# Attention and a routed expert layer on one core: the row steps of attention stand ahead of a task's products with V

## The chip, the cores and the metric
The kernel runs on one core of a Trainium2 chip. Its engines take their instructions from queues of their own and wait for each other through semaphores: TensorE (PE, matmuls; PEld its weight loads), VectorE (DVE), ScalarE (ACT), GpSimd (POOL) and SyncE (SP, which only issues DMAs here). The metric is the time of one execution on the device, in microseconds. Before the change the median of 3 runs is 685.51 us (685.28 to 686.04).

## The reference
Eight batches of 576 tokens and 8 heads of 64. The first four heads see the last 32 tokens, the other four every 32nd token. The rows of all batches, 4608 by 512, then go through a layer of 8 experts of which each token takes one.

```
scores = scale * np.matmul(q, k.transpose(0, 1, 3, 2))
mask_local = (rel >= 0) & (rel < stride)
mask_strided = (rel >= 0) & (pos[None, :] % stride == pos[:, None] % stride)
...
attn = np.exp(scores)
attn = attn / (np.sum(attn, axis=-1, keepdims=True) + 1e-09)
return np.matmul(attn, v).astype(np.float32)
...
logits = x @ w_gate
expert_idx = np.argmax(logits, axis=1)
...
    h = np.maximum(xe @ w1[e], 0.0)
    ye = h @ w2[e]
    out[mask] = gate_w[mask, None] * ye
```

## The kernel before
The work of attention is cut into 40 tasks (b, k): batch b of 8, bank k of 5. A bank is one PSUM bank that holds the scores of four pairs of blocks. Banks 0 and 1 are local heads, bank 3 and 4 strided ones, bank 2 has both. A loop over i works on three tasks at once: `stage_s` of task i (mask and scores, L354, L360, L369, then the softmax: maximum L316, subtraction L319, exponential L320, sum L322, reciprocal L324 and L325, and the normalization on GpSimd, L326), `stage_t` of task i − 2 (four transposes of the probabilities, L396, and a copy `pT`), and the products with V of task i − 3, where its bank completes something: `av_local` behind bank 1, `av_strided` behind banks 3 and 4 (L406). ScalarE copies the products into `xT`, the rows of x transposed (L113).

Two batches are a group of 9 blocks of 128 tokens. Behind the products of bank 4 of a batch, row steps go into a list: `logits` of each chunk of 384 tokens that is now complete (one behind the first batch of a group, two behind the second; L468, then transposes L475 and the gate, L476 to L490), `xrows` of each block (four transposes L460, a copy, a store to `xd` by ScalarE's queue, L463, with the gate that GpSimd copies beside it, L457), and behind the second batch `route` of the group: counts on TensorE (L508, L510), place and key of every token, two factors `am` and `bb` on VectorE (L534, L542, L544), and their product, L549, which adds the tokens' numbers to `idacc`. Each pass of the loop takes three steps from the list, in its last lines. In the list of group 2, behind `route`, stands `start_early`: three gathers (L184) of expert 0's first rows, so that its work may begin while the last group is routed.

The engines' queues are filled by a scheduler. It takes what the program issued first as the more urgent, and moves an instruction ahead of others where it expects the inputs of these later. So the place in the loop decides the order in the main, and not to the letter. PSUM banks `s` (scores, logits, rows of x, counts) are three that go round, `t` two, `v` three. Behind the loop, TensorE's order is written out by hand: the logits of the last group between the transposes and first matmuls of expert 0 (L220, L234 to L253). The experts' weights come in f32 and are split in two parts by ScalarE (L165) and VectorE (`wlo`, L166); from there on TensorE works through the experts to the end.

Of the kernel before, what the change touches and what calls it, by code (L numbers as in the profile page):

```python
# [43 lines left out]
LAG_AV = 3  # L44
# [45 lines left out]
def moe_attn(ctx, tc, lqk, vl, sqk, vs, wg, wcat, blob, out):  # L90
# [10 lines left out]
    def bank(tag):  # L101
        if tag in rings:
            rings[tag].append(rings[tag].pop(0))
            tag = rings[tag][-1]
        return ps.tile([128, 512], F32, name=tag)

    def evac(which, out, in_):
        if which == "v":
            nc.vector.tensor_copy(out=out, in_=in_)
        elif which == "g":  # L110
            nc.gpsimd.tensor_copy(out=out, in_=in_)
        else:
            nc.scalar.copy(out=out, in_=in_)  # L113
# [173 lines left out]
    with ExitStack() as actx:  # L287
# [43 lines left out]
        def load_l(b, hp):  # L331
            qk = inp.tile([128, LW], F32, name="lqk_sb")
            loaded[b, "l", hp] = qk
            nc.sync.dma_start(out=qk, in_=lqk[b, hp])

        def load_s(b, hp):
            qk = whl.tile([128, CHW], F32R, name="whi").bitcast(F32)[:, 0:2 * S]
            loaded[b, "s", hp] = qk
            nc.sync.dma_start(out=qk, in_=sqk[b, hp])

        def load_vl(b, hp):
            vt = inv.tile([128, NQB // 2, 128], F32, name="vt", bufs=3)
            loaded[b, "vl", hp] = vt
            nc.sync.dma_start(out=vt, in_=vl[b, :, hp])

        def load_vs(b):
            vst = inv.tile([128, NRG, 128], F32, name="vst")
            loaded[b, "vs"] = vst
            nc.sync.dma_start(out=vst, in_=vs[b])
# [43 lines left out]
        def stage_t(b, k, prob):  # L393
            tb = bank("t")
            for x in range(4):
                nc.tensor.transpose(tb[:, x * 128:(x + 1) * 128], prob[:, x * 128:(x + 1) * 128], ident)  # L396
            pT = pts.tile([128, 512], F32, name="pT")
            evac("a", pT, tb)
            pTs[b, k] = pT
# [8 lines left out]
        def av_local(b, xT, off):  # L408
            vt = [loaded[b, "vl", hp] for hp in range(2)]
            av = [bank("v"), bank("v")]  # L410
            for hp in range(2):
                for m in range(4):
                    for i in range(2):
                        n = 2 * m + i
                        for y in range(2):
                            for h in range(2):
                                av_mm(av[y], 256 * hp + QB * n, QB, h, y, vt[hp][64 * y:64 * y + 64, n, 64 * h:64 * h + 64],
                                      probs_of(b, ("l", hp, m), y, slice(64 * h + 32 * i, 64 * h + 32 * i + 32)))
            for y in range(2):
                dst = xT[:, 0:2, off:off + 512].rearrange("p a (n y q) -> p a n y q", y=2, q=QB)[:, :, :, y, :]  # L420
                evac("a", dst, av[y].rearrange("p (a n q) -> p a n q", a=2, q=QB))
# [43 lines left out]
        def logits(g, c3, xT, L):  # L465
            lb = bank(LTAG)
            for pr in range(4):
                nc.tensor.matmul(lb[32 * pr:32 * pr + 32, 0:384], wg_sb[:, pr, :], xT[:, pr, c3 * 384:(c3 + 1) * 384],  # L468
                                 start=True, stop=True, tile_position=(0, 32 * pr))
            ls = rt.tile([128, 384], F32, name="ls", bufs=2)  # L470
            evac(LS_ENG, ls, lb[:, 0:384])
            yield
            lt = bank(LTAG)
            for i in range(3):
                nc.tensor.transpose(lt[:, i * 128:(i + 1) * 128], ls[:, i * 128:(i + 1) * 128], ident)  # L475
            nc.vector.tensor_reduce(out=L[:, 3 * c3:3 * c3 + 3, :],  # L476
                                    in_=lt[:, 0:384].rearrange("p (t q e) -> p t e q", t=3, q=4)[:, :, 0:E, :],
                                    axis=AX.X, op=ALU.add)
            cs = slice(3 * c3, 3 * c3 + 3)
            mx = rt.tile([128, 3], F32, name="mx", bufs=2)  # L480
            nc.vector.tensor_reduce(out=mx, in_=L[:, cs, :], axis=AX.X, op=ALU.max)
            dl = dls[g][:, cs, :]
            nc.vector.tensor_tensor(out=dl, in0=L[:, cs, :], in1=mx.unsqueeze(2).broadcast_to([128, 3, E]), op=ALU.subtract)
            ex = rt.tile([128, 3, E], F32, name="ex", bufs=2)
            nc.scalar.activation(out=ex, in_=dl, func=AF.Exp)
            yield
            gt = gates[g][:, cs]
            nc.vector.tensor_reduce(out=gt, in_=ex, axis=AX.X, op=ALU.add)
            nc.vector.tensor_scalar(out=gt, in0=gt, scalar1=1e-9, scalar2=None, op0=ALU.add)
            nc.vector.reciprocal(out=gt, in_=gt)  # L490
# [85 lines left out]
        def one(fn, *a):  # L576
            fn(*a)
            yield

        def step():  # L580
            while queue:
                try:
                    next(queue[0])
                    return True
                except StopIteration:
                    queue.pop(0)
            return False
# [23 lines left out]
        nt = len(tasks)  # L611
        pvs = {}
        for i in range(nt + LAG_AV):
            if i < nt:
                b, k = tasks[i]
                pvs[i] = stage_s(b, k)
                if b + 1 < B:
                    if k in (0, 1):
                        load_l(b + 1, k)
                    elif k in (3, 4):  # L620
                        load_s(b + 1, k - 3)
            it = i - LAG_T
            if 0 <= it < nt:
                stage_t(*tasks[it], pvs.pop(it))
            ia = i - LAG_AV
            if 0 <= ia < nt:
                b, k = tasks[ia]
                g, bb = divmod(b, GB)
                if g not in xTs:
                    xTs[g] = xtp.tile([128, 4, GB * S], F32, name="xT")  # L630
                    Ls[g] = rt.tile([128, GT, E], F32, name="L", bufs=2)
                    dls[g] = rt.tile([128, GT, E], F32, name="dl", bufs=2)
                    gates[g] = rt.tile([128, GT], F32, name="gt", bufs=2)
                if k == 1:
                    av_local(b, xTs[g], bb * S)
                elif k == 3:
                    av_strided(b, 0, xTs[g], bb * S)
                    if b + 1 < B:
                        load_vl(b + 1, 0)
                        load_vl(b + 1, 1)  # L640
                elif k == 4:
                    av_strided(b, 1, xTs[g], bb * S)
                    if b + 1 < B:
                        load_vs(b + 1)
                    for c3 in range(bb, 1 if bb == 0 else GT // 3):
                        queue.append(logits(g, c3, xTs[g], Ls[g]))
                    for c in range(3 * bb, 3 if bb == 0 else GT):
                        queue.append(one(xrows, g, c, xTs[g]))
                    if bb == GB - 1:
                        queue.append(route(g))  # L650
                        if g == NG - 2:
                            queue.append(one(start_early))
            if i < nt + LAG_AV - 1:
                for _ in range(3):
                    step()
        early = holder[0]
        lga, lgb = queue[0:2]
        rows = queue[2:8]
# [310 lines left out]
def build(nc, tc, aps):  # L969
    moe_attn(tc, *[aps[n] for n in _INS], aps["out"])  # L970
# [20 lines left out]
```

## Time and profile before

| | |
|---|---|
| median of 3 runs | 685.51 us |
| the profiled execution | 689.96 us, span 688.2 us |
| TensorE busy, mean granted clock | 641.9 us (93%), 0.967 |
| VectorE, ScalarE, GpSimd busy | 405.5, 319.1, 142.7 us |
| attention | 0 to some 201 us; the experts after it |

The page gives busy times over the whole span; the table of stretches gives them by stage, with the clock that TensorE was granted (1.00 is 2.4 GHz, and the other of its two levels is half of it). In the order of time a row is a run of equal instructions: start, length, engine, line, what it writes and reads, how many, and in brackets the idle time of the engine before it and what ended that. A bracket with "issue" is idle time that ended with no semaphore that the profile shows. Matmuls overlap, so rows of TensorE may overlap too.

### The profile page before, as it was taken

The numbers are of one execution on the slowest core, as the hardware profiler recorded it, in microseconds if no ns is written. First come the engines' busy times: TensorE is split into PE (matmuls) and PEld (weight loads), VectorE is DVE, ScalarE is ACT, GpSimd is POOL, SyncE is SP. The second block draws the span as 40 slices with busy tenths as digits, with TensorE's granted clock in tenths as the row PEclk, the third lists the DMA queues.
The fourth block names the chain that finished last, engine by engine and source line by source line (L and its number), as shares of the span: only waits on it lengthen the run. The fifth ranks groups of instructions, "written<-read, shape, count | busy, mean of one in ns | idle before, by whom it ended". The sixth has DMA issues, their size and how long they took to land.

```text
span 688.2 us, 15915 instructions
## 1 busy us (share of the span) xinstructions
PE 641.9 (93%) x6692; PEld 523.0 (76%) x6692; DVE 405.5 (59%) x762; ACT 319.1 (46%) x537; POOL 142.7 (21%) x163
## 2 busy tenths in 40 slices
PE   4898799899879999999999999999999999999992
PEld 3665677668659888888888888888888888888881
DVE  4564767867947984466646656456565556543320
ACT  1353545656733633355545455545555455534220
POOL 1321222332413060231123103301240124001102
PEclk9797999999989999999999999999999999999996
DMA  9386976776245674655575646654675566312301
GB/s 344 137 268 242 326 272 231 272 273 207 84 169 185 267 264 144 215 210 196 195 258 192 228 168 253 230 213 163 231 257 196 183 230 232 117 62 81 106 0 62
DMA packets 30217, 137.01 MB, mean 199 GB/s; under 512 B 4669, under 2 KB 4669, under 8 KB 21440
## 3 DMA queue, kind: packets, MB, share of 16 engines
q1 hardware_dynamic: 17856, 105.65, 43.0%
q0 software_dynamic: 6432, 20.26, 8.6%
q10 hardware_dynamic: 5856, 10.07, 3.9%
q8 instruction: 53, 0.87, 0.5%
q14 instruction: 20, 0.16, 0.1%
HBM read 116.79 MB, written 20.22 MB: 199 GB/s over the span
## 4 chain that ended last, share of the span: by engine, by line
PE 52%; issue 13%; DVE 6%; POOL 2%; ACT 1%; ACTq 0%; POOLq 0%; DVEq 0%
PE t L236 6%; PE t L234 6%; PE t L235 6%; PE s L253 4%; PE s L251 4%; PE s L252 4%; PE t L787 2%; PE t L788 2%; PE t L786 2%; DVE wlo L166 2%; PE v L815 2%; PE v L814 2%; PE v L816 2%; POOL out_dram L203 2%; PE v L253 1%
## 5 line engine op out<-in xcount | busy, mean ns | idle before, releaser
L166 DVE TENSOR_TENSOR wlo<-raw,whi 128x1024 fp32r<-128x1024 f32 x136 | 161.8, 1221 | 86.5 <-ACT whi L165 86.5
L165 ACT CAST whi<-raw 128x1024 fp32r<-128x1024 f32 x136 | 138.0, 1049 | 85.1 <-PE v L816 38.3
L234 PE MATMUL t<-xh,whi 128*128 128x512 f32 (+1 forms) x256 | 100.8, 394 | 0.0
L236 PE MATMUL t<-xh,wlo 128*128 128x512 f32 (+1 forms) x256 | 98.8, 386 | 0.6 <-DVE wlo L166 0.6
L235 PE MATMUL t<-xl,whi 128*128 128x512 f32 (+1 forms) x256 | 98.3, 384 | 0.0
L240 ACT ACTIVATE hh<-t 128x512 fp32r<-128x512 f32 (+1 forms) x64 | 37.4, 585 | 116.3 <-PE t L236 114.6
L241 DVE SCALAR_TENSOR_TENSOR hl<-t,hh 128x512 fp32r<-128x512 f32 (+1 forms) x64 | 43.0, 672 | 79.3 <-ACT hh L240 79.3
L251 PE MATMUL s<-whi,hh 128*128 128x512 f32 x176 | 71.4, 406 | 0.0
L253 PE MATMUL s<-whi,hl 128*128 128x512 f32 x176 | 69.3, 393 | 0.0
L252 PE MATMUL s<-wlo,hh 128*128 128x512 f32 x176 | 69.0, 392 | 0.0
L326 POOL TENSOR_TENSOR prob<-prob,ri 128x512 f32<-128x512 f32 x40 | 42.5, 1064 | 115.9 <-DVE ri L325 64.3
L184 POOL DMA_INDIRECT xg<-xd,ids x28 | 30.3, 1083 | 138.7 <-DVE gx L225 106.1
L203 POOL DMA_INDIRECT out_dram<-y,oids x28 | 35.5, 1266 | 107.5 <-ACT y L200 52.9
L236 PEld LDWEIGHTS t<-xh,wlo 128*128 128x128 f32 x256 | 48.0, 188 | 10.3 <-DVE wlo L166 1.0
L234 PEld LDWEIGHTS t<-xh,whi 128*128 128x128 f32 x256 | 48.1, 188 | 7.9 <-DVE xl L178 0.3
L235 PEld LDWEIGHTS t<-xl,whi 128*128 128x128 f32 x256 | 48.2, 188 | 7.7
L316 DVE TENSOR_REDUCE nm<-s 128x8 f32<-128x512 f32 x40 | 27.4, 686 | 26.4 <-PE s L360 19.4
L113 ACT COPY pT<-t 128x512 f32<-128x512 f32 x40 | 23.5, 587 | 37.5 <-PE t L396 35.6
L786 PE MATMUL t<-whi,sxh 128*128 128x256 f32 x144 | 40.7, 282 | 0.0
L787 PE MATMUL t<-wlo,sxh 128*128 128x256 f32 x144 | 40.2, 279 | 0.0
L788 PE MATMUL t<-whi,sxl 128*128 128x256 f32 x144 | 40.2, 279 | 0.0
L253 PEld LDWEIGHTS s<-whi,hl 128*128 128x128 f32 x176 | 33.0, 188 | 7.5
(165 smaller groups left out, 1174.5 us busy)
## 6 DMA issues: line engine op xcount, KB each, us to landing
raw<-in_wcat_dram SPq DMA_DIRECT2D x68, 1024.0 KB, 5.3
xd<-xr ACTq DMA_DIRECT2D x36, 264.0 KB, 3.5
lqk_sb<-in_lqk_dram SPq DMA_DIRECT2D x16, 592.0 KB, 6.2
whi<-in_sqk_dram SPq DMA_DIRECT2D x16, 576.0 KB, 4.1
vt<-in_vl_dram SPq DMA_DIRECT2D x16, 576.0 KB, 7.5
vst<-in_vs_dram SPq DMA_DIRECT2D x8, 704.0 KB, 7.9
xg<-xd,ids POOLq DMA_INDIRECT x28
out_dram<-y,oids POOLq DMA_INDIRECT x28
```

The source lines that it names most:

```text
L165: nc.scalar.copy(out=hi[:, sl], in_=raw[:, sl])
L166: i = nc.vector.tensor_tensor(out=lo[:, sl], in0=raw[:, sl], in1=hi[:, sl].bitcast(F32), op=ALU.subtract)
L203: lastp[0] = i = nc.gpsimd.indirect_dma_start(out=out, out_offset=bass.IndirectOffsetOnAxis(ap=idc, axis=0), in_=y, in_offset=None, bounds ...
L234: nc.tensor.matmul(hb[:, 0:n], whi[:, w], xh[:, dc, :], start=(dc == 0), stop=False)
L235: nc.tensor.matmul(hb[:, 0:n], whi[:, w], xl[:, dc, :], start=False, stop=False)
L236: nc.tensor.matmul(hb[:, 0:n], wlo[:, w], xh[:, dc, :], start=False, stop=(dc == 3))
L251: nc.tensor.matmul(yb[t], hh[:, ts], whi[:, w], start=(j == 0), stop=False)
L252: nc.tensor.matmul(yb[t], hh[:, ts], wlo[:, w], start=False, stop=False)
L253: nc.tensor.matmul(yb[t], hl[:, ts], whi[:, w], start=False, stop=(j == 7))
L786: nc.tensor.matmul(hb[:, 0:CW], xh[:, dc, :], whi[:, w], start=(dc == 0), stop=False)
L787: nc.tensor.matmul(hb[:, 0:CW], xh[:, dc, :], wlo[:, w], start=False, stop=False)
L788: nc.tensor.matmul(hb[:, 0:CW], xl[:, dc, :], whi[:, w], start=False, stop=(dc == 3))
```

## The change
The three row steps of each pass of the loop move ahead of the pass's products with V, and the condition that left them out of the last pass goes. A batch's steps are put into the list by the products of its bank 4, so its first ones now run in the pass after that.

```
@@ the loop of attention
             it = i - LAG_T
             if 0 <= it < nt:
                 stage_t(*tasks[it], pvs.pop(it))
+            for _ in range(3):
+                step()
             ia = i - LAG_AV
             if 0 <= ia < nt:
                 b, k = tasks[ia]
...
                         queue.append(route(g))
                         if g == NG - 2:
                             queue.append(one(start_early))
-            if i < nt + LAG_AV - 1:
-                for _ in range(3):
-                    step()
```

On TensorE, behind the products of task (3, 4), where `s0_1986` and `s2_2006` are the logits of two chunks and `t1_2044` the transposes of task (4, 1), the queue of the kernel before reads:

```order
L406 MATMUL v2_1955<-pT_1820,vst_1559 64x36 x2
L468 MATMUL s0_1986<-xT_1131,wg_sb_78 32x384 x2
L468 MATMUL s2_2006<-xT_1131,wg_sb_78 32x384
L468 MATMUL s0_1986<-xT_1131,wg_sb_78 32x384 x2
L468 MATMUL s2_2006<-xT_1131,wg_sb_78 32x384 x3
L396 MATMUL t1_2044<-cst_70,prob_1858 128x128 x4
L406 MATMUL v0_2124<-pT_1952,vt_1910 64x32 x2
L406 MATMUL v1_2125<-pT_1952,vt_1910 64x32
L396 MATMUL t0_2117<-cst_70,prob_1938 128x128
L475 MATMUL s1_1993<-cst_70,ls_1991 128x128 x3
```

In the changed kernel the same place on TensorE reads as follows; `s0_1986` is now the scores of task (4, 3), `s1_2024` and `s0_2044` are the logits:

```order
L406 MATMUL v2_1955<-pT_1802,vst_1559 64x36 x2
L354 LDWEIGHTS identb_71
L354 MATMUL s0_1986<-mask_b_79,identb_71 128x512
L369 MATMUL s0_1986<-whi_1590 54x54 x8
L369 MATMUL s0_1986<-whi_1590 36x36 x2
L369 MATMUL s0_1986<-whi_1633 36x36 x2
L369 MATMUL s0_1986<-whi_1633 54x54 x4
L396 MATMUL t1_2017<-cst_70,prob_1858 128x128 x4
L468 MATMUL s1_2024<-xT_1131,wg_sb_78 32x384 x4
L396 MATMUL t0_2086<-cst_70,prob_1938 128x128 x4
L406 MATMUL v0_2124<-pT_1952,vt_1910 64x32
L468 MATMUL s0_2044<-xT_1131,wg_sb_78 32x384
```

The scores of bank 3 and the transposes of bank 1 have moved ahead of the logits, and the first chunk's four matmuls stand together; the second chunk's come one matmul ahead of the transposes of the first chunk's logits.

Behind the products of task (4, 4), the index products of a group (L549, of the factors `am` and `bb`) stand on TensorE before the change directly behind the transposes of bank 1 of the next batch:

```order
L369 MATMUL s1_2486<-whi_2115 54x54 x4
L396 MATMUL t0_2517<-cst_70,prob_2340 128x128 x4
L549 LDWEIGHTS am_2407
L549 MATMUL s2_2524<-bb_2483,am_2407 128x64
L549 LDWEIGHTS am_2407
```

In the changed kernel TensorE has there:

```order
L369 MATMUL s1_2481<-whi_2084 54x54 x4
L396 MATMUL t0_2512<-cst_70,prob_2309 128x128 x4
L354 LDWEIGHTS identb_71
L354 MATMUL s2_2524<-mask_b_79,identb_71 128x512
L369 MATMUL s2_2524<-whi_2084 54x54 x16
L406 MATMUL v0_2602<-pT_2434,vt_2392 64x32 x2
L406 MATMUL v1_2603<-pT_2434,vt_2392 64x32 x2
L406 MATMUL v0_2602<-pT_2434,vt_2392 64x32 x2
L406 MATMUL v1_2603<-pT_2434,vt_2392 64x32
L549 LDWEIGHTS am_2447
```

The scores of bank 4 (`s2_2524`) and seven products with V have moved ahead of the index products.

At the end of attention, GpSimd before the change has the normalizations of the last four tasks between the early gathers (`xg`):

```order
L326 TENSOR_TENSOR prob_3258<-prob_3258,ri_3263 128x512
L184 DMA xg_3456<-xd_69,eids_85 128x528
L326 TENSOR_TENSOR prob_3349<-prob_3349,ri_3354 128x512
L184 DMA xg_3458<-xd_69,eids_85 128x528
L326 TENSOR_TENSOR prob_3422<-prob_3422,ri_3427 128x512
L184 DMA xg_3460<-xd_69,eids_85 128x528
L326 TENSOR_TENSOR prob_3499<-prob_3499,ri_3504 128x512
```

In the changed kernel GpSimd has:

```order
L326 TENSOR_TENSOR prob_3227<-prob_3227,ri_3232 128x512
L326 TENSOR_TENSOR prob_3336<-prob_3336,ri_3341 128x512
L326 TENSOR_TENSOR prob_3417<-prob_3417,ri_3422 128x512
L326 TENSOR_TENSOR prob_3458<-prob_3458,ri_3463 128x512
L184 DMA xg_3492<-xd_69,eids_85 128x528
L184 DMA xg_3494<-xd_69,eids_85 128x528
L184 DMA xg_3496<-xd_69,eids_85 128x528
```

All three gathers now stand behind the last normalization.

## Rows read from the trace of the kernel before

**Rows 1.** The page: TensorE's busy time; its granted clock in 40 slices.

```profile
PE 641.9 (93%) x6692; PEld 523.0 (76%) x6692; DVE 405.5 (59%) x762; ACT 319.1 (46%) x537; POOL 142.7 (21%) x163
...
PEclk9797999999989999999999999999999999999996
```

**Rows 2.** Table of stretches: length, busy time and count by engine, clock, DMA share, GB/s.

```profile
37.20:62.50 25.30, 21.08 (x519) 15.44 (x512) 13.31 (x35) 11.46 (x25) 6.27 (x9) 0.87 0.87 311
...
109.30:151.10 41.80, 38.76 (x1074) 29.14 (x1066) 31.90 (x91) 23.71 (x52) 11.81 (x19) 1.00 0.75 266
...
174.90:201.00 26.10, 21.16 (x345) 13.25 (x346) 16.82 (x37) 13.29 (x28) 8.92 (x10) 0.80 0.45 144
201.00:677.00 476.00, 472.98 (x2462) 398.68 (x2462) 273.61 (x408) 221.29 (x329) 89.66 (x83) 1.00 0.52 185
```

**Rows 3.** Order of time, TensorE: logits; start, length, what, count, idle before.

```profile
38.70 0.83 PE L468 MATMUL s<-xT,wg_sb 128*32 128x384 f32 x2 [0.28 <-ACT xT L113]
...
62.52 4.06 PE L468 MATMUL s<-xT,wg_sb 128*32 128x384 f32 x16
...
92.64 0.85 PE L468 MATMUL s<-xT,wg_sb 128*32 128x384 f32 x8
...
109.31 3.46 PE L468 MATMUL s<-xT,wg_sb 128*32 128x384 f32 x16
...
151.12 3.60 PE L468 MATMUL s<-xT,wg_sb 128*32 128x384 f32 x16
```

**Rows 4.** Order of time, all engines, 109.5 to 112.5: normalizations and copies of xT.

```profile
109.74 1.04 POOL L326 TENSOR_TENSOR prob<-prob,ri 128x512 f32<-128x512 f32 x1 [1.90 <-DVE ri L325]
110.03 1.21 ACT L113 COPY xT<-v 128x270 f32<-128x270 f32 x4
...
111.46 1.04 POOL L326 TENSOR_TENSOR prob<-prob,ri 128x512 f32<-128x512 f32 x1 [0.68 <-DVE ri L325]
```

**Rows 5.** Order of time, TensorE, 130 to 180: transposes, scores, logits.

```profile
134.02 0.66 PE L396 MATMUL t<-cst,prob 128*128 128x128 f32 x4 [1.25 <-POOL prob L326]
...
146.66 0.60 PE L396 MATMUL t<-cst,prob 128*128 128x128 f32 x4 [0.82 <-issue]
...
173.07 0.96 PE L369 MATMUL s<-whi 64*54 64x54 f32 x32
175.52 1.07 PE L396 MATMUL t<-cst,prob 128*128 128x128 f32 x4 [1.49 <-POOL prob L326]
...
177.00 1.51 PE L468 MATMUL s<-xT,wg_sb 128*32 128x384 f32 x8
...
178.98 0.96 PE L369 MATMUL s<-whi 64*54 64x54 f32 x30
```

**Rows 6.** Order of time, VectorE, 167 to 177: first count, a subtraction, last factor.

```profile
167.10 0.23 DVE L513 TENSOR_TENSOR rk<-s,cnt 128x72 f32<-128x72 f32 x1
...
174.17 0.64 DVE L319 TENSOR_TENSOR prob<-s,nm 128x512 f32<-128x512 f32 x1
...
175.70 0.50 DVE L544 TENSOR_SCALAR bb<-bm,cst 128x288 bf16<-128x288 f32 x1
```

**Rows 7.** Order of time, all engines, 173 to 195: the end of attention.

```profile
181.94 0.99 POOL L184 DMA_INDIRECT xg<-xd,eids  x1 [0.16 <-issue]
...
183.98 1.21 DVE L166 TENSOR_TENSOR wlo<-raw,whi 128x1024 fp32r<-128x1024 f32 x1
184.17 1.88 POOL L184 DMA_INDIRECT xg<-xd,eids  x1 [0.16 <-issue]
...
188.35 1.19 DVE L166 TENSOR_TENSOR wlo<-raw,whi 128x1024 fp32r<-128x1024 f32 x1
188.56 1.88 POOL L326 TENSOR_TENSOR prob<-prob,ri 128x512 f32<-128x512 f32 x1 [2.52 <-DVE gt L490]
...
193.91 1.19 ACT L113 COPY xT<-v 128x270 f32<-128x270 f32 x4 [1.36 <-PE v L406]
```

**Rows 8.** Order of time, TensorE: a pause among the products with V.

```profile
86.05 0.30 PE L406 MATMUL v<-pT,vt 64*64 64x32 f32 x4 [3.01 <-issue]
```

More of the change, by code (lines that the diff above doesn't have):

```diff
@@ L624, in moe_attn @@
                 stage_t(*tasks[it], pvs.pop(it))
+            for _ in range(3):
+                step()
             ia = i - LAG_AV
@@ L652, in moe_attn @@
                             queue.append(one(start_early))
-            if i < nt + LAG_AV - 1:
-                for _ in range(3):
-                    step()
         early = holder[0]
```

## The prediction, made before the changed kernel was run

> **What bounds the kernel now.** I read the page first, then a table of stretches, then the order of time on TensorE, then the other engines where TensorE waits. On the page TensorE is busy in 93% of the span, but its clock is below full only in the first 200 us and at the end [rows 1]. The table says why that matters: from 201 to 677 us (the experts) TensorE is busy 472.98 of 476 us at clock 1.00, so nothing there can be had or lost by this change, which touches only attention; whatever attention ends earlier or later arrives at the end one for one. In attention TensorE is busy 38.76 of 41.80 us in an undisturbed stretch of two batches (109.3 to 151.1) and 21.16 of 26.10 us at its end (174.9 to 201), there at a mean clock of 0.80 [rows 2]. Since a busy TensorE is not one at its peak, I look for rows that take longer than the same work elsewhere.
>
> There is one kind. Eight logit matmul instructions (one chunk of 384 tokens) take 0.85 us when they stand together; the sixteen of two chunks take 4.06, 3.46 and 3.60 us at the three places where a second batch of a pair ends, against 1.70 for two chunks [rows 3]. They come right behind the products of bank 4, and need x transposed, which ScalarE copies out of PSUM from 110.03 to 111.24 [rows 4]; moreover the scheduler interleaved both chunks as their inputs come, and so broke the four that run side by side. After batch 0 the one chunk is in three pieces, one with a wait of 0.28 [rows 3].
>
> Three further waits of TensorE are for probabilities: 1.25 us at 134.02, 0.82 at 146.66, 1.49 at 175.52 [rows 5].
>
> **What the change removes, adds and moves.** No instruction is added or removed. On TensorE the scores of bank 3 and a transpose now stand between the products of bank 4 and the logits; route's counts and index products stand one task later; SyncE's second load of strided keys goes ahead of loads of V; GpSimd does the last four normalizations before the early gathers.
>
> *A, logits of two chunks (three places).* I take 109.3 as the model. To gain: 3.46 − 1.70 = 1.76. Behind the products, which end at 109.3, the new order has the scores of (4,3), 0.96 behind some 0.35 of mask [rows 5], to 110.65; a transpose that needs a normalization finished at 109.74 + 1.04 = 110.78 [rows 4], so 0.13 wait; to 111.45. The copies of xT ended at 111.24, so the first chunk waits for nothing, to 112.30. The next transpose needs the normalization that ends at 112.50: 0.20. Then the transposes of the logits want VectorE's copy of the first chunk, which now queues behind a maximum and a subtraction of (4,3); about 0.1 is left of that, an estimate from the 0.64 of one subtraction [rows 6]. 1.76 − 0.43 = 1.3. The bounds: 0 if VectorE is later by more, 1.8 if no wait is left. Three places: −3.9 us (0 to −5.4).
>
> *B, the chunk after batch 0.* Two pieces too many of 0.83, and the 0.28: −1.9 at best [rows 3]. But from 37.2 to 62.5 the DMA engines are 87% busy [rows 2], and data may be late next. I take −0.6, a third (0 to −1.9).
>
> *C, the routing halves of pairs 1 and 2.* Here the change puts a wait in. VectorE's list from the first count to the end of both index factors took 167.10 to 176.20 = 9.1 us; the new order has one subtraction (0.64) less in it, so 8.4 [rows 6]. It starts when the counts are done, about 1.5 us after the scores of bank 1 (an estimate: two transposes, one x row and the counts); those end some 6.9 us ahead of the end of the scores of bank 3. So the factors are ready at 8.4 − 5.4 = 3.0 us after the scores of bank 3. TensorE is there after a transpose (0.66), the scores of bank 4 (1.3) and 7 products, at 2.2: 0.9 wait for the index products. What queues behind it is the transpose of bank 2, whose normalization now ends at 3.0 + 0.2 + 1.04 + hops = 4.4, while TensorE comes at 3.7: 0.7 more. So 1.6 in each of the two pairs, 3.2; the old waits there are 1.25 + 0.82 (pair 2 alone) = 2.07. Sum +1.1 us (−2.0 if VectorE is ahead, +2.5 if both pairs lose a further microsecond of wait).
>
> *D, the end of attention.* Time 0 is the end of the scores of (7,3), 173.07 + 0.96 = 174.03 [rows 5]. Before, the last copies of xT end at 193.91 + 1.19 = 195.10 [rows 7], at +21.1. The long item there is the last normalization: it waits behind two gathers and VectorE's weight subtractions and ends at 190.44. After: index products at +3.0, the last two normalizations end at +8.6 and +9.7, the gathers only then. VectorE's first two weight subtractions end at +12.3, the gate's exponential on ScalarE, which stands ahead of the copies of xT, at +12.8; copies for bank 3 to +14.0, the products of bank 4 to about +14.3. Gates are ready at +15.1. Three gathers at 0.99 to 1.88 each plus 0.16 between end at +13.3 to +15.9, the gate copies behind them at +15.6 to +16.4; ScalarE holds its last xT copies behind the three stores of x rows that wait for those gate copies: two copies 1.2, issues 1.0, xT 1.2. So +19.0 to +19.8, where it was +21.1: −1.5 (−2.8 to +0.5). The gathered rows are back by then: the gathers end 3 us before they are needed.
>
> The last normalization took 1.88 us beside a weight subtraction of 1.19, where others take 1.04; and a gather took 1.88 beside one that had begun 0.19 us earlier, against 0.99 [rows 7]. The Trainium skill (page "SBUF — State Buffer", section "Who interferes with whom") says that a VectorE instruction with two SBUF inputs shuts out a GpSimd one that reads SBUF, but that generating a gather's descriptors should not be shut out by it. The first agrees with the row, the second does not. By the page the gathers would all take 0.99 and D would be −2.1 rather than −1.5.
>
> *E, pauses that no wait explains.* TensorE stands still for 3.01 us ahead of 86.05 [rows 8], with no releaser; of that kind there are seven from 1.3 us up in attention, where many short matmuls follow one another. Work packed closer gives them less cover. I charge +1.2, an estimate of a third of that largest one (−1.5 to +4).
>
> Loads: SyncE's are swapped by one place. Each swapped load has two tasks or more until it is used, some 9 us; I cost that at nothing, and if the cover is gone it shows as a pause of E's size.
>
> Sum −3.9 − 0.6 + 1.1 − 1.5 + 1.2 = −3.7 us. The profiled execution took 689.96 us (688.2 of span and 1.8 around); it would become 686.3. The median of the runs shown is 685.51, 4.45 lower; the same difference gives 681.8.
>
> **The rivals.**
> *1, no change.* VectorE keeps attention's pace, and what the logits give back is waited for again at the index products. For: C's chain is VectorE's, and it is busy 31.90 of 41.80 us [rows 2], more of it in the routing half. Against: in the logits' stretch it idles. Time: A halved to −1.9, C at its bad end of +2.5, D, B and E as they are: −0.3, 685.2.
> *2, slower: the new pair of waits lets the clock fall.* Place: the index products after batches 2, 4 and 6. At 175.52, behind a wait of 1.49, four transposes took 1.07 us (0.66 at 134.02, where the wait was 1.25), and eight logit instructions 1.51 at 177.00 (0.85 at full clock) [rows 3, 5]: TensorE ran at 1.2 of 2.4 GHz for some 3.4 us, until the scores at 178.98. [...] Price: 3.4 us at half speed lose 1.7. Twice 1.7 for pairs 1 and 2, C at +2.5, A at half: −1.9 − 0.6 + 2.5 − 1.5 + 1.2 + 3.4 = +3.1, 688.6. Against: the two waits are 0.65 us of work apart, and the 1.25 did not do it.
> The Trainium skill (page "TensorE: Matmul & The Clock Gate", section "What's actually happening") has the clock halve after idling, which agrees with 175.52; by the same rule rival 3 gains.
> *3, clearly faster.* The waits that let the clock fall at 175.5 and in the end (0.80 from 174.9 to 201, 0.87 from 37.2 to 62.5 [rows 2]) go with this order. One half-speed stretch less is −1.7, two −3.4: 680.1 to 678.4.
> *4, the change doesn't do what it says:* the scheduler undoes it. Excluded by the order, which shows the logits behind the scores at all places.
>
> **How the numbers follow.** Forecast (−1.5 to −5.5 us) 0.48, rival 3 0.20, rival 1 0.16, rival 2 0.16. About 0.2%, 1.4 us, is what a measurement of this kernel can tell from no change. Faster 0.67 (forecast and rival 3, less a little of the forecast's edge, with a little of rival 1), same 0.16, slower 0.17. The range that leaves out 2 in 10: 677.0 to 687.5; the forecast's own is 680.0 to 684.0.
>
> **What would show it right or wrong.** A: logits in rows of 0.85 per chunk, and no row of 3.4 us behind bank 4's products. C: a wait of TensorE for VectorE's factors ahead of the index products, of about 0.9 us. D: the last normalization without its 1.88, gathers behind it, last copies of xT 19 to 20 us after the scores of (7,3). Wrong if TensorE's time between the ends of two pairs stays at 41.8 us, if new half-speed stretches stand behind the index products, or if the first expert matmul comes no earlier than at 201.5.

## The result, and the profile after

The changed kernel takes 696.66 us (692.25 to 698.88, 6 runs) against 685.50 (684.65 to 690.72): 1.0149 of before, 95% interval 1.0115 to 1.0183. It was forecast at 681.8 and is slower by 1.5%. Its profiled execution has a span of 697.0 us, where before had 688.2: the two profiles show 8.8 of the 11.2 us between the medians. The page of the changed kernel, TensorE's busy time and its clock in 40 slices, for [rows 1]:

```profile
PE 641.3 (92%) x6686; PEld 526.6 (76%) x6692; DVE 402.8 (58%) x762; ACT 320.3 (46%) x537; POOL 143.3 (21%) x163
...
PEclk9797999899979999999999999999999999999997
```

TensorE has the same work, and is no busier. The table of stretches of the changed kernel, at the times of [rows 2] (length, busy time and count by engine, clock, DMA share, GB/s):

```profile
37.20:62.50 25.30, 20.91 (x556) 16.50 (x551) 14.07 (x36) 13.11 (x30) 6.73 (x9) 0.81 0.83 312
109.30:151.10 41.80, 33.62 (x875) 25.61 (x870) 26.94 (x82) 19.53 (x44) 10.79 (x18) 0.92 0.69 244
174.90:201.00 26.10, 20.34 (x584) 16.11 (x584) 21.31 (x54) 18.78 (x40) 10.49 (x11) 0.97 0.45 147
201.00:677.00 476.00, 473.14 (x2461) 396.99 (x2460) 273.86 (x410) 221.15 (x331) 86.65 (x79) 0.99 0.53 187
```

The second row is the one to read: in the stretch that was undisturbed before, TensorE is busy for 5 us less, and its clock is 0.92 where it was 1.00. The first matmul of expert 0 comes at 210.48 us, 9.0 later than before (201.50), and the experts take what they took: all of the loss arises ahead of it. To find where, I take four marks, VectorE's maximum (L316) of tasks (3,3), (5,3) and (7,3), and the first expert matmul (L234); the times between them, in us:

```
                          to (3,3)  (3,3)-(5,3)  (5,3)-(7,3)  (7,3)-L234
before                       91.9      42.7         41.5        25.4
after                        90.4      50.6         43.8        25.7
```

Up to (3,3) the changed kernel is 1.5 us ahead, in the two batches after that it loses 7.9. What stands there is in the order of time on TensorE, changed kernel (start, length, engine, line, what, count, idle time before and what ended it):

```profile
97.48 1.02 PE L360 MATMUL s<-lqk_sb 64*32 64x64 f32 x57
101.18 0.43 PE L360 MATMUL s<-lqk_sb 64*32 64x64 f32 x7 [2.68 <-issue]
...
126.73 0.90 PE L360 MATMUL s<-lqk_sb 64*32 64x64 f32 x25 [3.83 <-issue]
...
150.37 0.98 PE L360 MATMUL s<-lqk_sb 64*32 64x64 f32 x55 [1.93 <-issue]
```

These are pauses like the one of [rows 8]: in the midst of one task's scores, with no releaser. Behind them the clock falls. The stretch around the longest, first before, then after:

```profile
119.00:132.00 13.00, 12.48 (x411) 10.11 (x405) 10.04 (x31) 8.22 (x17) 3.59 (x6) 1.00 0.71 251
```

```profile
119.00:132.00 13.00, 9.17 (x235) 8.02 (x238) 4.70 (x20) 5.28 (x10) 1.98 (x7) 0.74 0.50 164
```

**What a pause is.** Cut the changed kernel's time at the ends of its pauses and count (TensorE's matmuls and weight loads, the first two counts):

```profile
51.88:57.80 5.92, 4.78 (x127) 3.99 (x128) 2.85 (x6) 2.32 (x6) 1.04 (x1) 0.58 0.85 318
...
77.81:83.45 5.64, 3.33 (x128) 2.88 (x128) 4.34 (x15) 1.69 (x3) 1.20 (x2) 1.00 0.88 300
83.45:101.16 17.71, 13.81 (x381) 10.62 (x381) 10.33 (x29) 7.60 (x18) 4.64 (x7) 0.89 0.76 263
101.16:126.70 25.54, 21.04 (x508) 15.24 (x510) 14.28 (x43) 11.67 (x26) 5.95 (x10) 0.90 0.63 213
```

The sums are 255, 256, 762 and 1018, that is 1, 1, 3 and 4 times 256 with a few instructions that no count holds. So pauses of this kind, without a releaser, stand only at every 256th of TensorE's instructions. The page of either kernel has a DMA queue for it, "q8 instruction: 53, 0.87" (packets, MB): 16 KB each, 53 blocks for 13,384 matmuls and weight loads. The DMA view of the changed kernel, first ahead of the pause (119.6 to 122.7 us) and then in it (122.4 to 126.8), in 40 slices, and the queues' shares:

```profile
DMA  0040739899899979997999959979859996999699
...
q1 hardware_dynamic: 212, 0.99, 94.6%
```

```profile
DMA  9995959599998999998864441101010000010010
...
q10 hardware_dynamic: 286, 0.54, 32.2%
q1 hardware_dynamic: 71, 0.31, 22.1%
q8 instruction: 1, 0.02, 1.3%
```

The block's packet is carried at 124.28 us, when the loads issued before it have drained, and TensorE goes on 2.4 us later, at 126.73. TensorE had entered the block before at 119.63. Between the two times the DMA engines carried 1.22 MB of SyncE's loads (q1) and 0.30 MB of the stores of x rows (q10), which ScalarE issued at 120.33 and 121.36. These stores are row steps too; no experiment moves them alone. At each pause over 1 us, in both traces, the time from the packet to TensorE's next instruction is 2.2 to 2.5 us; the packet itself is carried 2.5 to 4.7 us after TensorE entered the block before, and TensorE ran through the 256 short matmuls and weight loads ahead of the pauses at 83.47 and 126.73 in 3.3 us. So a block is late when many loads were issued shortly ahead of it and the block before it is one of short matmuls. The Trainium skill (page "Runtime: NRT & Kernel Launch", section "Instruction fetch mechanics") has instructions refilled in blocks of 256 by a DMA queue of their own; that agrees. It also has the cost of a block's end as mostly hidden; here it is up to 3.83 us, and the measurement decides.

Why the new order meets it: the scores of (3,3) and (3,4) were 5.5 us apart (maxima at 91.91 and 97.40), and are 1.8 apart now (90.40, 92.16), since the logits stand behind them. Both release a tile of keys, so SyncE issues four loads (keys, keys, V, strided V, 2.4 MB) between 89.0 and 92.3 us, where before they went out between 91.6 and 97.2. And of the second batch of a pair, the second load of keys went ahead of the strided V (118.22 and 118.60 us together; before 115.43 for V, 118.61 for keys).

**The rest, by the prediction's steps.** Logits of two chunks of the changed kernel, at the second place, for [rows 3]:

```profile
111.66 1.94 PE L468 MATMUL s<-xT,wg_sb 128*32 128x384 f32 x8
...
114.83 0.83 PE L468 MATMUL s<-xT,wg_sb 128*32 128x384 f32 x2
...
116.07 0.85 PE L468 MATMUL s<-xT,wg_sb 128*32 128x384 f32 x6
```

The index products and the transpose behind them, for [rows 5]:

```profile
91.63 0.42 PE L549 MATMUL s<-bb,am 128*128 128x64 bf16 x9 [0.42 <-DVE bb L544]
...
92.95 0.66 PE L396 MATMUL t<-cst,prob 128*128 128x128 f32 x4 [0.55 <-POOL prob L326]
...
142.23 0.42 PE L549 MATMUL s<-bb,am 128*128 128x64 bf16 x9 [0.93 <-DVE bb L544]
...
143.55 0.66 PE L396 MATMUL t<-cst,prob 128*128 128x128 f32 x4 [0.55 <-POOL prob L326]
```

And the end of attention, for [rows 7]; GpSimd first:

```profile
192.55 1.88 POOL L184 DMA_INDIRECT xg<-xd,eids  x1 [0.15 <-issue]
194.74 2.02 POOL L184 DMA_INDIRECT xg<-xd,eids  x1 [0.31 <-issue]
197.06 0.95 POOL L184 DMA_INDIRECT xg<-xd,eids  x1 [0.30 <-issue]
```

```profile
200.72 2.04 PE L468 MATMUL s<-xT,wg_sb 128*32 128x384 f32 x4 [3.39 <-ACT xT L113]
202.69 0.69 PE L220 MATMUL t<-cst,xg 128*128 128x128 f32 x2
205.29 0.47 PE L220 MATMUL t<-cst,xg 128*128 128x128 f32 x1 [1.91 <-DMA xg<-xd,eids]
```

The gathers end at 198.0, but the rows of the second and third arrive at 201.8 and 205.2: SyncE issued two weight loads of 1 MB at 194.76 and 197.20, between them.

### The profile page after: what moved, and what is told of

The parts are those of the page before. It is cut to its first block, busy times and chain, and to the rows that moved or that the text cites. A ratio compares the mean times of both kernels' runs of the same rounds, so it can differ in the third digit from the quotient of the medians.

```text
span 697.0 us, 15912 instructions
## 1 busy us (share of the span) xinstructions
PE 641.3 (92%) x6686; PEld 526.6 (76%) x6692; DVE 402.8 (58%) x762; ACT 320.3 (46%) x537; POOL 143.3 (21%) x163
## 4 chain that ended last, share of the span: by engine, by line
PE 66%; issue 16%; DVE 9%; POOL 4%; DMA 2%; ACT 1%; POOLq 0%; ACTq 0%; DVEq 0%
PE t L236 6%; PE t L234 6%; PE t L235 6%; PE s L253 4%; PE s L251 4%; PE s L252 4%; PE v L406 3%; PE s L360 3%; PE t L396 3%; PE s L460 2%; PE t L787 2%; PE t L786 2%; PE t L785 2%; PE v L814 2%; PE v L813 2%
## 5 line engine op out<-in xcount | busy, mean ns | idle before, releaser
L234 PE MATMUL t<-xh,whi 128*128 128x512 f32 (+1 forms) x256 | 100.8, 394 | 0.2 <-DVE xl L178 0.2
L236 PEld LDWEIGHTS t<-xh,wlo 128*128 128x128 f32 x256 | 48.1, 188 | 10.2 <-DVE wlo L166 1.0
L234 PEld LDWEIGHTS t<-xh,whi 128*128 128x128 f32 x256 | 48.1, 188 | 8.0 <-DVE xl L178 0.4
L316 DVE TENSOR_REDUCE nm<-s 128x8 f32<-128x512 f32 x40 | 27.2, 680 | 34.9 <-PE s L360 26.1
L360 PE MATMUL s<-lqk_sb 64*32 64x64 f32 x1152 | 25.9, 239 | 15.4 <-issue 15.4
```

What stands on the lines that cost most here:

```text
L234: nc.tensor.matmul(hb[:, 0:n], whi[:, w], xh[:, dc, :], start=(dc == 0), stop=False)
L236: nc.tensor.matmul(hb[:, 0:n], wlo[:, w], xh[:, dc, :], start=False, stop=(dc == 3))
L360: nc.tensor.matmul(sb[o:o + QB, col:col + 64], qk[hs, QB * j:QB * j + QB], qk[hs, S + QB * j:S + QB * j + 64], start=False, stop=last, til ...
```

## The experiments

Theory 1: late blocks of instructions behind loads, and the clock behind each pause, make the loss. Theory 2: the new order's own waits do. In all experiments but the two padded ones TensorE has attention's instructions in the order of the kernel they start from; only a few neighbouring products with V change places. Ratios are to the kernel before on the same chip.

**Two weight loads late.** Each of them stood beside the pauses before 90 us.

```
+ i = nc.sync.dma_start(out=raw, ...)
+ # chunk 0: issue_after(i, load of keys (7,0)); chunk 1: issue_after(i, load of V (7,1))
```

> Kernel before the change, but the first two 1 MB loads of expert weights (raw), which SyncE issues at some 48 and 73 us, wait in its queue until the loads of the last batch (about 157 and 170 us). Nothing else moves. Theory 1, TensorE's own instructions come late: every 256 instructions TensorE needs a new block, fetched by DMA, and the fetch stands behind whatever loads were issued before it. Then the pauses at 52.86 (2.3 us), 59.45 (1.7), 79.86 (1.4) and 86.05 us (3.0), which lie beside these two loads, shrink to under 1 us each, and the half-clock stretches from 52.7, 59.6 and 86.9 us go at least in part: 4 to 12 us faster. Theory 2, the pauses are slack that waits on other engines would fill anyway: within 1.5 us of 685.5. Theory 3, the loads are late for the weight casts at the end of attention: 1 to 5 us slower.

> The changed kernel with the same two loads late. Theory 1: the pauses at 51.90 (2.6 us), 57.82 (0.8), 77.83 (1.0) and 83.47 us (2.3) shrink, those at 101.18 (2.9), 126.73 (3.8) and 150.37 us (1.9), which have no raw load beside them, stay or move: 3 to 10 us faster than 696.7. Theory 2: within 1.5 us of 696.7. Theory 3: slower.

Measured: 1.0017 (0.9986 to 1.0048) and 1.0175 (1.0119 to 1.0230). By the total Theory 1 missed; the profile says why. Of the kernel before, three of the four pauses by the old places fell under 0.5 us (the first stayed, 2.67 us at 51.25), two of 1.04 and 1.24 us came at later blocks, and the scores of (6,4) came 8.8 us sooner; but the moved load made a new pause (raw_late_before, TensorE):

```profile
156.66 0.30 PE L406 MATMUL v<-pT,vt 64*64 64x32 f32 x3 [3.18 <-issue]
```

Between the maxima of (6,4) and (7,3), around this pause, 4.4 of the 8.8 us were lost again. The profiled execution, one of the fastest of 12, keeps the rest; their median does not show it. In the changed kernel the three pauses with no weight load beside them stayed, as Theory 1 had it (3.57 us at 98.40, 3.73 at 124.74, 2.22 at 148.09), and one of 3.15 us came at 177.16. Where a load is moved to, its bytes can delay another block.

**The blocks shifted.** 192 and 128 instructions of TensorE more, at 14 us.

```
+ if i == 3: m matmuls of 4 columns into an unread PSUM bank (2 instructions each)
```

> The changed kernel with 192 more TensorE instructions (96 matmuls of 4 columns into a PSUM bank that nothing reads) at about 14 us, where TensorE waits for loads; the order of all other instructions on all engines is the same. Theory 1 (blocks of 256 instructions fetched behind loads): every later instruction stands 192 places further on, the ends of blocks fall elsewhere. The pauses at 101.18, 126.73 and 150.37 us (2.9, 3.8 and 1.9 us) go or move; worked out from the backlog of loads in the trace the stretch from 85 us on has some 3 us of them instead of 8.5. 3 to 9 us faster than the changed kernel (696.7). Theory 2 (the new order's own waits make it slow): within 1 us of it, pauses where they were.

> The kernel before with 128 such instructions at the same place. Theory 1: pauses at other places; by the backlog of loads some 6 us from 85 us on instead of 3.7: 1 to 6 us slower than before. Theory 2: within 1 us of it.

Measured: 1.0130 (1.0097 to 1.0162) and 1.0081 (1.0053 to 1.0109). The pauses moved, in pad192_after to these places (TensorE, the first three behind 90 us):

```profile
94.32 0.42 PE L406 MATMUL v<-pT,vt 64*64 64x32 f32 x12 [1.23 <-issue]
...
101.47 0.31 PE L406 MATMUL v<-pT,vt 64*64 64x32 f32 x6 [2.64 <-issue]
...
128.96 0.86 PE L360 MATMUL s<-lqk_sb 64*32 64x64 f32 x44 [1.21 <-issue]
```

They stand at other matmuls than before, again at multiples of 256. So the place in the count makes the pause and no wait of these instructions; that is shown. By the time Theory 1 is not borne out. The padding, with a pause of 1.8 to 2.0 us in it at 16 us, makes both kernels some 5 us late by the maximum of (1,3), so the total of padb128_before falls into the forecast of 1 to 6 us slower for another reason: behind 85 us its pauses over 0.5 us add up to 3.8 us, not to the 6 expected. From (3,3) to (5,3) pad192_after took 46.6 us, for 50.6.

**The weight loads in quiet stretches.**

```
+ i == 6: load_vl(1, 0), moved up; raw tile of chunk 0; nc.gpsimd.tensor_copy(raw[0:1, 0:1], prob of (0,4)); its load
+ chunk 1: issue_after(i, load of V (7,1))
```

> The kernel before with the first 1 MB load of weights in the quiet stretch of the DMA engines at 27 to 34 us, behind a small copy of GpSimd (one element) that holds it back until TensorE has asked for its next two blocks, and the second at 166 us, behind the last load of attention. With both late, attention ran 8.8 us ahead at the scores of (6,4), and lost 4.4 of them to a pause of 3.4 at 156.66, beside the first of them. Theory 1: the 8.8 stay, 6 to 10 us faster than before. Rival: the pause comes back elsewhere, as long as the load's 1 MB stands somewhere in the queues: within 2 us.

> The changed kernel with the same two loads at the same places. Theory 1: it keeps its pauses at some 98, 124 and 148 us (8 us in all), which have no weight load beside them, and so stays 7 us or more behind raw_split_before; against the changed kernel 2 to 5 us faster. Rival: both kernels come to the same time within 2 us, so that the weights' loads alone made the difference.

Measured: 0.9929 (0.9892 to 0.9965), faster than before by 4.4 us of the expected 6 to 10, and 1.0106 (1.0042 to 1.0171). The changed kernel kept pauses of 4.52, 3.55 and 1.85 us at 100.30, 125.68 and 149.85 us, as Theory 1 had it.

**The loads' order.** Restored in the changed kernel, and the new one put into the kernel before; SyncE's queue alone differs.

```
loads_back_after, b >= 3:  + load_vs(b + 1); load_s(b + 1, 1)     (was: load_s in the pass of (b, 4))
swap_before, b > 3:        + issue_after(load_vs(b), load_s(b, 1))
```

> The changed kernel, but from batch 4 on SyncE's second load of strided keys of a batch stands again behind the load of strided V, as in the kernel before; nothing else moves on any engine. Theory 1a: what made the changed kernel slow is this swap, by which two loads of 1.28 MB together are issued right ahead of a block's fetch. At 118.2 us only the keys (576 KB) are then in front of the fetch asked for at 119.66: the pause at 126.73 falls from 3.9 us to under 1, and its two half-clock slices go; 3 to 8 us faster than the changed kernel (696.5 on this chip). The pauses at 101.2 and 150.4 stay nearly (the same four loads are issued within 3 us there in any order). Theory 1b: pauses are a lottery of block ends and loads, no order of the loads is better: within 2 us. Theory 2 (waits of the new order): within 1 us, the pause at 126.73 replaced by another wait.

> The kernel before, with that swap alone: from batch 4 on the load of strided V stands behind the second load of strided keys, and nothing else moves. Theory 1a: the fetch asked for at 97.38 us then has 1.28 MB more in front of it (+3 to 4 us at 102.1), that at 142.4 about 2 us more, with the half-clock slices behind them: 3 to 9 us slower than before, without any row step moved. Theories 1b and 2: within 2 us.

> The changed kernel with the loads' order restored and with the two early weight loads placed at 27 and 166 us. Theory 1a: the sum of both, 4 to 10 us faster than the changed kernel, still behind raw_split_before (683.8) by the pauses at 101 and 150 (some 5 us and their clock). Theory 2: it stays at 696.

Measured: 1.0123 (1.0090 to 1.0157), 1.0065 (1.0033 to 1.0098) and 1.0078 (1.0035 to 1.0120). The swap alone makes the kernel before 0.65% slower, with no row step moved. Its profile was taken of its fastest execution (687.51 us) and doesn't show where. Undoing the swap gives little back, no more than Theory 1b allows (within 2 us), and by the intervals 1.0123 is not told apart from the 1.0149 of the changed kernel: the pause at 126 fell to 2.13 us, not under 1, and that at 101 stayed (loads_back_after, TensorE):

```profile
101.72 0.44 PE L360 MATMUL s<-lqk_sb 64*32 64x64 f32 x7 [3.23 <-issue]
...
126.46 0.55 PE L360 MATMUL s<-lqk_sb 64*32 64x64 f32 x25 [2.13 <-issue]
```

**Without the loads of V.**

```
(from raw_split_before, raw_split_after)
+ vt = loaded[0, "vl", hp] if b else inv.tile(...)      # the same for vst; no DMA for b > 0
```

> raw_split_before without the loads of V from batch 1 on (some 13 MB of the loads of attention): the tiles of batch 0 are used for all batches, so the values of the products are others, and with them the routing and the experts' shares; the order of instructions on all engines but SyncE is the same. Read by the first matmul of expert 0, not by the total. Theory 1: hardly a pause of over 0.5 us is left, the first expert matmul comes at 185 to 191 us (raw_split_before: 194.7, with 11 us of pauses, most of them before 60 us).

> The same for the changed kernel. Theory 1 (the row steps' new place is good in itself and its gain is lost to late blocks of instructions): with the backlog of loads gone, the pauses at 98, 124 and 148 us are gone too, and the first expert matmul comes 1 to 5 us earlier than in no_v_before, as the terms A to D of the prediction have it. Theory 2 (the new order waits more in itself): it comes 3 to 10 us later, as with all loads (raw_split_after: 211.7 against 194.7).

The first expert matmul came at 190.51 and 192.16 us; Theory 1 had the changed kernel 1 to 5 ahead, Theory 2 had it 3 to 10 behind. Neither came: with the loads gone 17.0 us of difference (raw_split, 194.67 and 211.71) shrink to 1.65. So in these two profiles the new order without those loads costs no more than that; the rest of the 17.0 needs the loads. Pauses over 1 us were left in both, 2.52 us at 51.46 in the kernel before, and 1.10, 1.44, 1.96 and 1.21 us at 28.37, 33.32, 110.54 and 157.62 in the changed one. The products have other values here, so the experts get other shares and the totals (749.45 and 750.77) don't compare with the other runs.

**The fourth load paced.**

```
(from loads_back_after)
+ in load_s(b + 1, 1), b >= 3: nc.gpsimd.tensor_copy(out=qk[0:1, 0:1], in_=prob of (b, 4)[0:1, 0:1])
```

> loads_back_after, and from batch 4 on the second load of strided keys also waits for a copy of one element by GpSimd, some microseconds after the scores that free its tile; the order on all other engines is the same. In the changed kernel the scores of banks 3 and 4 of a batch stand 1.8 us apart (5.5 before), so the loads of four tiles go out within 3 us right ahead of a block's fetch. Theory 1: with the fourth one later, the fetches asked for at some 95, 120 and 144 us have 0.6 to 0.7 MB less in front of them: the pauses at 101.7, 126.5 and 148.5 (3.3, 2.2, 0.5 us in loads_back_after) fall to under 1.2 us each and their half-clock slices go, from the maximum of task (3,3) to that of (5,3) it takes 43 to 46 us (48.8; 50.6 in the changed kernel; 42.7 before): 3 to 7 us faster than the changed kernel. Theory 2 (the new order's own waits): 48 us or more, within 2 us of loads_back_after.

> The same with the two early weight loads at 27 and 166 us, as in raw_split_before. Theory 1: with both sources of backlog gone the changed order comes to 682 to 688, level with raw_split_before within 3 us; whether the row steps' new place then gains or loses a little, this tells. Theory 2: 690 or more.

Measured: 1.0050 (1.0028 to 1.0073) and 1.0040 (1.0002 to 1.0078). From (3,3) to (5,3) it takes 44.1 us in paced_after, as expected. Its pauses there:

```profile
103.23 0.43 PE L406 MATMUL v<-pT,vt 64*64 64x32 f32 x16 [1.76 <-issue]
...
119.33 0.55 PE L360 MATMUL s<-lqk_sb 64*32 64x64 f32 x25 [0.74 <-issue]
```

The pause of 1.76 us is over the 1.2 expected. Restoring the order and holding back one load of four by some microseconds gives back two thirds of what the change lost (1.0149 to 1.0050). paced_split_after, at 690.82 us, is not in Theory 1's 682 to 688 but in Theory 2's 690 or more; some cost stays when these loads are moved.

**The weight loads behind the gathers.**

```
+ chunk 2: nc.gpsimd.tensor_copy(out=raw[0:1, 0:1], in_=cst[0:1, 0:1])     # behind the third gather
```

> The changed kernel, and the third load of expert weights (194.8 us there, between the early gathers at 192.6, 194.7 and 197.1) waits for a copy of one element that GpSimd does behind the third gather; the fourth load follows it on SyncE's queue. Nothing else moves. If the gathered rows are late because 2 MB of weights stand in front of them (landed at 201.8 and 205.2 us, 7 and 8 us after their issue, and TensorE waits for the last until 205.3), they land by 202 us: the first expert matmul comes 2 to 4 us sooner after the scores of (7,3) (28.3 us in the changed kernel, from the maximum of (7,3) 25.7), and the kernel is 1 to 4 us faster than the changed one. Rival: the x rows that go into the gather, or the logits at half clock, hold the end: within 1 us.

> paced_after with the same hold on the third weight load. If both causes add up: 1 to 4 us faster than paced_after (690.6, 1.005 of before), so within 0.3% of the kernel before, or a little faster.

Measured: 1.0074 (1.0043 to 1.0106) and 0.9999 (0.9970 to 1.0029). From (7,3) to the first expert matmul it takes 23.2 and 23.3 us, for 25.7, and the transposes of the gathered rows wait for no DMA (tail_after, TensorE):

```profile
200.86 0.90 PE L220 MATMUL t<-cst,xg 128*128 128x128 f32 x3
201.69 1.51 PE L468 MATMUL s<-xT,wg_sb 128*32 128x384 f32 x8
```

With the loads' order restored and two holds the changed order is level with the kernel before as it was.

**Both kernels with their loads put right.**

> The changed kernel with all three moves of loads: the fourth key load paced, the third weight load behind the gathers, the two early weight loads at 27 and 166 us. If the late blocks were all that the new place of the row steps cost, it is now 2 to 5 us faster than the kernel before with its loads put right (raw_split_before, 0.993 of before), by the end of attention (23.2 us from the maximum of (7,3) against 24.9) and the logits: 0.982 to 0.990 of before. If the place itself is worth nothing: 0.990 to 0.997. If it costs: over 0.997.

> The kernel before with the early weight loads moved as in raw_split_before and its key loads paced like those of paced_after. There the loads are already further apart, pauses from 85 us on are small but for 1.6 us at 96: 0 to 2 us faster than raw_split_before (0.990 to 0.993 of before).

Measured: 1.0012 (0.9985 to 1.0040) and 0.9895 (0.9842 to 0.9947). The last has the lowest median of the study, 681.26 us in 4 runs against 686.83 on the same chip; by the intervals it is not told apart from raw_split_before (0.9929). With these moves on both sides the new place of the row steps still costs 0.9% (by the medians) to 1.2% (by the ratios). That is no price of the place alone, since late blocks are left on both sides: here the changed order keeps one of 3.32 us at 77.18, where the largest near it in the other kernel is 1.29 us at 75.61. The profile of the changed order shows one more place (tail_paced_split_after, TensorE, then stretches):

```profile
88.98 0.42 PE L549 MATMUL s<-bb,am 128*128 128x64 bf16 x9 [0.95 <-DVE bb L544]
89.33 0.42 PE L406 MATMUL v<-pT,vt 64*64 64x32 f32 x12
90.30 0.66 PE L396 MATMUL t<-cst,prob 128*128 128x128 f32 x4 [0.55 <-POOL prob L326]
...
134.75 0.42 PE L549 MATMUL s<-bb,am 128*128 128x64 bf16 x9 [1.02 <-DVE bb L544]
...
136.07 0.66 PE L396 MATMUL t<-cst,prob 128*128 128x128 f32 x4 [0.55 <-POOL prob L326]
```

```profile
81.20:91.40 10.20, 8.70 (x260) 6.76 (x256) 10.04 (x28) 5.31 (x14) 2.08 (x2) 1.00 0.82 301
91.40:101.60 10.20, 10.20 (x192) 8.33 (x186) 4.65 (x15) 3.54 (x8) 2.73 (x6) 0.50 0.51 174
134.70:144.70 10.00, 8.72 (x234) 6.53 (x236) 7.03 (x20) 4.97 (x11) 3.77 (x7) 1.00 0.66 233
```

Two waits of 1.5 us together, and then 10.2 us at a granted clock of 0.50, the lower of the two levels (1.2 GHz). But the next pair of the same execution, as long, is followed by 10 us at full clock. In tail_paced_after the same pair (1.12 and 0.55) at 133.7 is followed by 3.5 us at half clock; in the changed kernel itself the pair at 142.23 is not, nor are those of no_v_after (0.66, 0.98 and 1.05, with 0.55 each), where the clock is 1.00 for 10 us behind each. So the pair is not always followed by the low clock, and no run takes it away: whether it makes part of the 0.9 to 1.2% stays open.

## Why the prediction was wrong

*A was mis-sized.* The logits took 4.06 + 3.46 + 3.60 = 11.1 us at the three places [rows 3] and take 2.53 + 3.62 + 3.22 = 9.4 now: 1.75 of the 3.9 forecast. What failed there is "the first chunk waits for nothing": I had ScalarE's copies of xT end at 111.24, as before. An exponential stands ahead of them in both kernels; in the new order it waits 0.99 us for VectorE's subtraction and starts at 110.96 instead of 109.50. So the copies end at 112.70, and the first chunk waits in the midst: 1.94 us for 0.85 at the second place, 1.54 at the third. And the second chunk stands in two rows at all three places, 0.83 and 0.85 us, where I had counted one of 0.85; that takes 2.5 us of the forecast.

*B was better than said:* one row of 0.85 us at 39.55 for the three pieces, about 1.9 for 0.6.

*C was right in its mechanism; that its size came out is luck.* The waits are 0.42 + 0.55 and 0.93 + 0.55 us by the rows, 2.45 in all, where I had 0.9 + 0.7 twice, 3.2. Against them I set old waits of 1.25 and 0.82. The second is no wait for probabilities: its row says "issue", the normalization was done at 144.42, 1.4 us before TensorE stopped, and the place is 9 times 256 instructions behind the pause at 102.11 (2296 counted, some are missing in the trace). So C is 2.45 − 1.25 = +1.2 where the forecast was +1.1, by two errors against each other.

*D was right in its mechanism and wrong in one sentence,* "the gathered rows are back by then: the gathers end 3 us before they are needed". The last copies of xT ended 18.2 us after the scores of (7,3) (183.01 to 201.22), for 19.0 to 19.8 forecast and 21.1 before. But a gather's end on GpSimd is the issue of a transfer. Beside 2 MB of weights the last rows came 7 us after that end, and what was won was waited for again: from the scores of (7,3) to the first expert matmul it takes 27.5 us in both kernels. tail_after shows it: with those loads behind, the end is 2.4 to 2.5 us shorter.

*E and the loads are the step that failed.* I saw the pauses (six from 1.3 us up, not seven), charged 1.2 us for them and gave their cause as cover ("work packed closer gives them less cover"); of the loads I wrote "I cost that at nothing, and if the cover is gone it shows as a pause of E's size". It did, three times. From 90 us on the pauses over 1 us make 2.68 + 3.83 + 1.93 + 1.02 = 9.5 us, for 1.3 before. At their places (94 to 105, 119 to 132 and 143 to 156 us) the clock is 0.84, 0.74 and 0.87 for 1.00 in all three before, which is worth another 1.8 + 3.4 + 1.7 = 6.9 us at most, part of it inside the pauses. Bounded at +4 for E, no case of mine held that. Moving loads alone takes the changed kernel from 1.0149 to 0.9999 (tail_paced_after). What was missing is the count: the trace of before already had its pauses 256, 768 and 1024 instructions apart, and the loads' backlog ahead of each.

*Rivals.* Rival 2 gave the right side and 688.6, by another mechanism; its own, half speed behind the pair of waits at the index products, is not in the changed kernel and only in some of the others. Of the signs that I named against me two came: the time between two pairs did not fall under 41.8 us (from index products to index products it is 50.6), and the first expert matmul came no earlier than 201.5. The new half-speed stretches came behind the pauses, not behind the index products.

## What to carry to other kernels

A pause of TensorE without a releaser, at every 256th instruction and beside full DMA queues, is a block of instructions that comes late: look at what was issued to the DMA queues since TensorE entered the block before and shortly ahead of that (here 2.5 to 4.7 us ahead of the block's packet), not at the engines. When a change moves the work that frees buffers closer together, the loads go out together too; count their bytes against the next block and against every small transfer (a gather, a row store) that is issued behind them. A load with time to spare can be held back by a one-element copy until the queues are quiet; where it goes instead has to be looked at as well, since the moved weight loads made new pauses of 3.18 and 3.15 us.

## What the runs showed of the hardware

Small transfers wait while bulk ones are under way on other queues: the early gathers landed 4.4, 7.0 and 8.2 us after their issue with two 1 MB loads among them, and 4.3 to 4.4 us with these behind. A block's fetch needs 2.2 to 2.5 us from its packet to TensorE's next instruction, at each pause over 1 us in the two kernels' traces.
